# Attention scores on two 64-row halves of the tensor array, three products each, in place of stacked queries and keys

## The chip, the cores and the metric

One core of a Trainium2 chip runs the whole program in one launch. The metric is the device time of one execution in microseconds (us). The kernel before was timed three times: 920.41, 920.97 and 925.29 us, median 920.97 us.

## The reference, cut to what matters

Three blocks follow one another. The change is in the first.

```python
def _attn_ref(q, k, v, w1, b1, w2):          # q, k, v: (4, 8, 576, 64)
    scores = scale * np.matmul(q, k.transpose(0, 1, 3, 2))
    ...                                      # bias[i, j, head] from a small network on positions
    scores = scores + bias.transpose(2, 0, 1)[None, :, :, :]
    scores = scores - np.max(scores, axis=-1, keepdims=True)
    attn = np.exp(scores)
    attn = attn / (np.sum(attn, axis=-1, keepdims=True) + 1e-09)
    return np.matmul(attn, v)

def _moe_ref(x, w1, w2, w3, w_out):          # x: (2304, 512), inner width 1024
    return ((x @ w1) * (x @ w2) @ w3) @ w_out

def _moe2_ref(x, w_in, w_out, g_ln):
    ...                                      # softmax-weighted hidden layer, layer norm, product
```

A score sums over 64 numbers, half the 128 rows of the tensor array. There are 4 x 8 = 32 pictures of 576 x 576 scores.

## The kernel before, in words

Every float32 operand of a product is split into a rounded part (hi) and a rest (lo) of the type float32r, and a product is made of hi·hi, hi·lo and lo·hi (`Chip.three`, lines 76 to 81).

**The stages.** `Bias.run` makes the bias table and stores it in DRAM (to about 59.7 us). `Attention` follows, then `Gated` (the first two-matrix block) and `Solu`. `Attention` works on 16 pairs `n`, each two heads of one batch, head pair outermost. One pair is 10 slots; `slot(s)` writes the instructions of slot `s`, pair `s // 10`, step `k = s % 10`. The engines work in the order in which slots write to them, so this order is a schedule by hand.

**One pair.** Nine units of 128 query rows are scored: unit 0 holds the last 64 rows of both heads ("ends"), units 1 to 4 the other rows of head 0, units 5 to 8 those of head 1. Per unit: scores into a two-bank PSUM tile `sp` (two buffers); `add_bias` on DVE (L381) reads `sp` and a bias tile `bt`, writes `e` and the row minimum; `exp` on ACT (L388); `inverse` on DVE (L395, L396); `normalise` on POOL (L400). `transposes` (L410) turns 128 x 128 blocks of `e` on PE into `tp`, or, for the piece called C, into an `sp` tile with a 128 x 64 array tile. ACT rounds the result (L484), DVE takes the rest (L498), and `values` (L453) multiplies by the values into `op`, which ACT copies out (L486) and SP stores to `x_d`. In slot `s` stand the scores of unit `k`, the transposes that lag by 8 slots (`LAG`) and the values that lag by 11.

**Preparation.** For the next pair, `prep` splits queries and keys on POOL: `qh` (L54), `ql` (L57), `kr` hi and lo (L54, L57), one step per slot in slots 0 to 3; steps 4 and 5 split the values in slots 5 and 6 of their own pair. SP then copies (`move`, L51) into stacked tiles: `q` holds, per head, qh over ql in 128 rows; `k` holds the head's keys twice. With those, one 128-row product sums two of the partial products, so a unit needs two products per half of 288 keys: hi keys and lo keys against the stack (L370), four in all:

```python
for half in range(2):
    for x in range(2):
        nc.tensor.matmul(
            ps[:, half, :HS], w["q"][:, h, q * 128 : q * 128 + 128], w["k"][:, h, x, half * HS : half * HS + HS],
            start=x == 0, stop=x == 1,
        )
```

The keys of head 1 are turned by 64 columns in the copy, since its scores lie turned in `e`. Unit 0 uses `qh`, `ql` and `kr` directly with `Chip.three`.

**After the last scores.** `tile_kernel` runs slots 160 to 174 with `ga.early(n)`, n = s - 160, beside them: weight conversions on ACT and DVE, loads of `x`, and the first products of `Gated` at n = 7, 10 and 14 (`EARLY`). At n = 8 (`MID`) the memory of `e` is given up and the second token chunk is loaded from `x_d` into it (16 DMAs `wf<-x_d`).

Of the kernel before, what the change touches and what calls it, by code (L numbers as in the profile page):

```python
# [17 lines left out]
S = 576  # L18
# [184 lines left out]
class Attention:  # L203
# [52 lines left out]
    def first_ab(self):  # L256

        chains = []
        wab = self.bp.tile([128, 2, S], F, tag="bt", name="wab", bufs=6)
        for f in range(2):  # L260
            x = wab[:, f, :DM]

            def out(f=f, x=x):
                if f == 0:
                    self.ga.first = self.ga.big(1)
                self.ch.load(self.ga.first[:, f].bitcast(F), x)

            chains.append(self.ch.f64_steps(self.ga.raw_ab[:, f].rearrange("p (n t) -> p n t", t=2), x) + [out])
        return [step for steps in zip(*chains) for step in steps]
# [10 lines left out]
    def load_qk(self, n):  # L280
        p, b = self.pairs[n]
        w = self.W.setdefault(n, {})
        w["qkr"] = self.qk.tile([128, 1216], F, tag="qkr", name="qkr")
        self.ch.load(w["qkr"], self.i["qk"][b, p])
# [7 lines left out]
    def prep(self, n, step, s):  # L292

        ch, w = self.ch, self.W[n]
        tl = lambda nm, sh, bufs=1: self.qk.tile(sh, R, tag=nm, name=nm, bufs=bufs)
        qr, kr = w["qkr"][:, :640], w["qkr"][:, 640:]

        def copies(dst, top, bottom):
            for h in range(2):
                r = slice(64 * h, 64 * h + 64)  # L300
                for d, src in ((dst[0:64, h], top[r]), (dst[64:128, h], bottom[r])):
                    self.at(s, lambda d=d, src=src: ch.move(d, src))

        def turned(dst, src):

            for h in range(2):
                r = slice(64 * h, 64 * h + 64)
                for a in (0, 64):
                    d = dst[a : a + 64, h]
                    for d, x in ((d[:, :, 64:], src[r, :, :512]), (d[:, :, :64], src[r, :, 512:])) if h else ((d, src[r]),):  # L310
                        self.at(s, lambda d=d, x=x: ch.move(d, x))

        if step == 0:
            w["qh"] = tl("qh", [128, 640])
            ch.pool_round(w["qh"], qr)
        elif step == 1:
            w["ql"] = tl("ql", [128, 640])
            ch.pool_rest(w["ql"], qr, w["qh"])
            w["q"] = tl("q", [128, 2, 512], 2)
            copies(w["q"], w["qh"][:, :512], w["ql"][:, :512])  # L320
        elif step == 2:
            w["kr"] = tl("kr", [128, 2, S])
            ch.pool_round(w["kr"][:, 0], kr)
        elif step == 3:
            ch.pool_rest(w["kr"][:, 1], kr, w["kr"][:, 0])
            w["k"] = tl("k", [128, 2, 2, S], 2)
            turned(w["k"], w["kr"])
        elif step == 4:
            w["v"] = self.ep.tile([128, 10, 128], R, tag="v", name="v", bufs=2)
            ch.pool_round(w["v"][:, :, 0:64], w["vr"])  # L330
        else:
            ch.pool_rest(w["v"][:, :, 64:128], w["vr"], w["v"][:, :, 0:64])

    def load_bias(self, p, *ks):
# [8 lines left out]
        if (p, "pair", pair) not in self.BT:  # L343
            self.BT[(p, "pair", pair)] = self.bp.tile([128, 2, S], F, tag="bt", name="bt", bufs=6)
# [10 lines left out]


    def scores(self, n, k):
        nc, w = self.nc, self.W[n]
        ps = self.sps.tile([128, 2, 512], F, tag="sp", name="sp")
        h, q = (1, k - 5) if k > 4 else (0, k - 1)  # L360
        if k == 0:

            for half in range(2):
                keys = [w["kr"][:, x, half * HS : half * HS + HS] for x in range(2)]
                self.ch.three(ps[:, half, :HS], [w[x][:, 512:640] for x in ("qh", "ql")], keys, True, True)
            e = w["eab"] = self.tp.tile([128, S], F, tag="eab", name="eab", bufs=2)
        else:
            for half in range(2):
                for x in range(2):
                    nc.tensor.matmul(  # L370
                        ps[:, half, :HS], w["q"][:, h, q * 128 : q * 128 + 128], w["k"][:, h, x, half * HS : half * HS + HS],
                        start=x == 0, stop=x == 1,
                    )
            if h == 0:
                w[("e", q)] = self.tp.tile([128, 2, S], F, tag="e", name="e", bufs=8)
            e = w[("e", q)][:, h]
        self.SQ[n * 10 + k] = (n, k, ps, e, self.st[(5 * n + k // 2) % len(self.st)])

    def add_bias(self, n, k, ps, e, st):

        self.nc.vector.tensor_tensor_reduce(  # L381
            out=halves(e), in0=ps[:, :, :HS], in1=halves(self.BT[(self.pairs[n][0], k)]), scale=-0.125, scalar=3e38,
            op0=ALU.add, op1=ALU.min, accum_out=st[:, k % 2 : k % 2 + 1],
        )

    def exp(self, n, k, ps, e, st):
        c = k % 2
        self.nc.scalar.activation(e, e, AF.Exp, bias=st[:, c : c + 1], scale=-1.0, accum_out=st[:, 2 + 2 * c : 3 + 2 * c])  # L388

    def inverse(self, n, k, ps, e, st):  # L390
        if k % 2 == 0 and k < 8:
            return
        c = 1 + k % 2
# [4 lines left out]
    def normalise(self, n, k, ps, e, st):  # L398
        c = 8 + k % 2
# [3 lines left out]
    def transposes(self, n, u):  # L403
# [7 lines left out]
        if u == "AB":  # L411
            for h in range(2):
                w[("et", h)] = [self.ep.tile([128, 4, S], R, tag="et" + x, name="et" + x, bufs=3) for x in "hl"]
            w["etl"] = [self.ep.tile([128, S], R, tag="el" + x, name="el" + x, bufs=2) for x in "hl"]
# [6 lines left out]
        elif u == "C":  # L421
            tr(0, w["eab"][:, 512:])
# [41 lines left out]
    TU = [["AB"], ["C", (0, 0)], [(0, 1)], [(0, 2)], [(0, 3)], ["L"], [(1, 0)], [(1, 1)], [(1, 2)], [(1, 3)]]  # L464
    AV = [(h, c) for h in range(2) for c in range(5)]

    def start(self, n):
        if n < 4:
            self.prep(0, n, -1)
        elif n == 4:  # L470
            self.load_qk(1)
        if n >= 5 and self.later[-1]:
            self.later[-1].pop(0)()

    def slots(self):
        return 10 * len(self.pairs) + self.LAG + 1 + self.AVLAG + 4

    def slot(self, s):
        NP = len(self.pairs)
        n, k = divmod(s, 10)  # L480
        SQ = self.SQ
# [5 lines left out]
        if s - 2 in SQ:  # L487
            self.exp(*SQ[s - 2])
        if s - 1 in SQ:
            self.add_bias(*SQ[s - 1])  # L490
        if s - 3 in SQ:
            self.inverse(*SQ[s - 3])
            if SQ[s - 3][1] % 2:
                self.normalise(*SQ[s - 4])
            if SQ[s - 3][1] % 2 or SQ[s - 3][1] == 8:
                self.normalise(*SQ[s - 3])
        for hi, lo, src in ev:
            self.nc.vector.tensor_tensor(out=lo, in0=src, in1=hi.bitcast(F), op=ALU.subtract)  # L498
        if n < NP and k < 9:
            self.scores(n, k)  # L500
        tn, tu = divmod(s - self.LAG, 10)
        if 0 <= tn < NP:
            for u in self.TU[tu]:
                self.transposes(tn, u)
        an, au = divmod(s - self.LAG - 1 - self.AVLAG, 10)
        if 0 <= an < NP:
            self.values(an, self.AV[au], s)
# [4 lines left out]
        if n < NP:  # L512
            if n + 1 < NP and k < 4:
                self.prep(n + 1, k, s + 1)
            if k in (5, 6):
                self.prep(n, k - 1, s + 1)
# [3 lines left out]
            if p + 1 < NPH:  # L520
                for j in self.AHEAD[min(p, 1)].get((b, k), ()):
# [811 lines left out]
```

## Time and profile before

| what | us |
|---|---|
| median of three runs | 920.97 |
| the profiled execution | 923.45 |
| its span, first to last instruction | 921.7 |
| PE busy in the span | 867.7 (94%) |
| PE weight loads (PEld) busy | 780.2 (85%) |
| DVE busy | 640.6 (70%) |
| ACT busy | 497.5 (54%) |
| POOL busy | 373.0 (40%) |

The shares are of the whole span. A stage has its own limits: between 150 and 300 us, in the middle of the attention, the 50-us windows show PE busy for 49.1 to 49.6 us. Products are pipelined, and a product's row is longer than its step to the next product. PEld is the loading of the stationary operand. Idle time of an engine is put down to what ended it.

### The profile page before, as it was taken

The page shows a single profiled execution, that of the slowest core. Times are in us where ns is not written, and L with a number is a line of the kernel's source. Part 1 is how long each engine was busy: PE and PEld are TensorE (multiplying, and loading weights), DVE is VectorE, ACT ScalarE, POOL GpSimd, SP SyncE. Part 2 cuts the span into 40 slices and gives each one's busy share as a digit, 9 for nine tenths or more (in the row PEclk, how much of TensorE's full clock was granted, in tenths as well). Part 3 has the DMA queues.
Part 4 walks back from the last instruction along what each step waited for, and adds up shares of the span by engine and source line. Part 5 has one row for each costly group of instructions (what it writes and reads, how often), then busy time and mean ns, then how long its engine had stood idle before and what let it go on. Part 6 is the DMA issues. An engine that isn't in the chain of part 4 may idle for free.

```text
span 921.7 us, 16129 instructions
## 1 busy us (share of the span) xinstructions
PE 867.7 (94%) x5430; PEld 780.2 (85%) x5430; DVE 640.6 (70%) x1481; ACT 497.5 (54%) x1052; POOL 373.0 (40%) x432
## 2 busy tenths in 40 slices
PE   7978998999999879979999998999999899999998
PEld 3448998999999769968889898999999688888886
DVE  8887997999999887986663396652445765555552
ACT  7876997899989844433322233232233544444432
POOL 2036887888888650020111024550343532222200
PEclk9997999999999998998999999999999999999999
DMA  6889899998997665654431486663324111111001
GB/s 229 291 281 227 225 269 228 245 276 227 263 285 184 199 197 194 233 204 155 159 115 35 162 284 195 219 215 96 90 89 134 45 46 46 47 46 47 24 23 47
DMA packets 98387, 151.56 MB, mean 164 GB/s; under 512 B 16384, under 2 KB 62848, under 8 KB 98304
## 3 DMA queue, kind: packets, MB, share of 16 engines
q1 hardware_dynamic: 91392, 141.09, 51.6%
q10 hardware_dynamic: 6912, 9.44, 2.9%
q8 instruction: 43, 0.70, 0.3%
q14 instruction: 40, 0.33, 0.1%
HBM read 81.40 MB, written 41.30 MB: 133 GB/s over the span
## 4 chain that ended last, share of the span: by engine, by line
PE 60%; DMA 11%; DVE 8%; SPq 6%; issue 3%; POOL 3%; ACT 3%; ACTq 0%; POOLq 0%; DVEq 0%
PE ab L79 6%; PE ab L80 6%; PE ab L81 6%; DMA k<-kr 4%; PE op L453 4%; SPq L51 4%; PE o L80 4%; PE o L79 4%; PE o L81 4%; PE sp L370 4%; PE x L80 3%; PE tp L410 3%; PE x L81 3%; PE x L79 3%; PE hx L79 2%
## 5 line engine op out<-in xcount | busy, mean ns | idle before, releaser
L79 PE MATMUL ab<-xh,ab 128*128 128x384 f32 x320 | 109.7, 343 | 6.6 <-DVE a L777 4.6
L80 PE MATMUL ab<-xl,ab 128*128 128x384 f32 x320 | 108.9, 340 | 0.0
L498 DVE TENSOR_TENSOR etl<-tp,eth 128x512 fp32r<-128x512 f32 (+1 forms) x160 | 99.4, 630 | 13.4 <-ACT eth L484 10.9
L81 PE MATMUL ab<-xh,ab 128*128 128x384 f32 x320 | 108.7, 340 | 0.0
L400 POOL TENSOR_SCALAR e<-e,st 128x576 f32<-128x576 f32 x128 | 95.4, 756 | 30.9 <-DVE st L396 28.7
L370 PE MATMUL sp<-k,q 128*128 128x288 f32 x512 | 91.9, 304 | 12.5 <-DMA k<-kr 5.9
L388 ACT ACTIVATE e<-e,st 128x576 f32<-128x576 f32 x128 | 100.2, 783 | 5.3 <-DVE st L381 5.2
L381 DVE CUSTOM_DVE_ANT_0 e<-sp,bt 128x576 f32<-128x576 f32 x128 | 95.6, 748 | 8.0 <-PE sp L370 6.4
L484 ACT CAST eth<-tp 128x512 fp32r<-128x512 f32 (+1 forms) x160 | 85.2, 543 | 26.5 <-PE tp L410 19.9
L410 PE MATMUL tp<-idt,e 128*128 128x128 f32 x576 | 88.9, 277 | 4.2 <-DVE ell L498 2.0
L729 POOL TENSOR_TENSOR xs<-xh,xl 128x384 f32<-128x384 f32 x20 | 23.0, 1162 | 172.0 <-DMA xl<-x_d 97.2
L370 PEld LDWEIGHTS sp<-k,q 128*128 128x128 f32 x512 | 77.1, 194 | 15.0 <-DVE st L381 6.3
L410 PEld LDWEIGHTS tp<-idt,e 128*128 128x128 f32 x576 | 70.8, 143 | 6.9 <-DVE ell L498 2.3
L80 PE MATMUL x<-gl,wf 128*128 128x384 f32 x192 | 66.5, 346 | 6.0 <-DVE gl L62 5.9
L79 PEld LDWEIGHTS ab<-xh,ab 128*128 128x128 f32 x320 | 61.1, 191 | 9.4 <-DVE a L777 6.3
L453 PE MATMUL op<-eth,v 128*128 128x288 f32 x256 | 66.3, 340 | 0.4 <-ACT o L486 0.4
L79 PE MATMUL x<-gh,wf 128*128 128x384 f32 x192 | 65.7, 342 | 0.0
L81 PE MATMUL x<-gh,wf 128*128 128x384 f32 x192 | 65.6, 342 | 0.0
L1157 POOL TENSOR_TENSOR st<-st,half 128x1 f32<-128x1 f32 x18 | 10.0, 554 | 131.9 <-DVE st L1156 131.9
L80 PEld LDWEIGHTS ab<-xl,ab 128*128 128x128 f32 x320 | 61.1, 191 | 0.4 <-DVE xl L738 0.4
L81 PEld LDWEIGHTS ab<-xh,ab 128*128 128x128 f32 x320 | 61.1, 191 | 0.0
L777 DVE TENSOR_TENSOR a<-ab,a 128x384 f32<-128x384 f32 x48 | 26.5, 552 | 47.9 <-ACT a L776 47.9
(207 smaller groups left out, 2288.3 us busy)
## 6 DMA issues: line engine op xcount, KB each, us to landing
bias_d<-rs SPq DMA_DIRECT2D x36, 295.5 KB, 4.2
qkr<-in_qk SPq DMA_DIRECT2D x16, 608.0 KB, 5.7
k<-kr SPq DMA_DIRECT2D x32, 288.0 KB, 6.6
x_d<-o SPq DMA_DIRECT2D x64, 144.0 KB, 4.1
g_d<-a ACTq DMA_DIRECT2D x48, 192.0 KB, 2.8
gl<-g_d SPq DMA_DIRECT2D x48, 192.0 KB, 2.7
k<-kr SPq DMA_DIRECT2D x32, 256.0 KB, 6.7
raw<-in_wo SPq DMA_DIRECT2D x16, 512.0 KB, 5.1
```

Of the source, the lines that this page charges most:

```text
L51: self.nc.sync.dma_start(out.bitcast(F), in_.bitcast(F))
L79: mm(out, a[0], b[0], start=first, stop=False, skip_group_check=more)
L80: mm(out, a[0], b[1], start=False, stop=False, skip_group_check=more)
L81: mm(out, a[1], b[0], start=False, stop=last, skip_group_check=more)
L370: nc.tensor.matmul(ps[:, half, :HS], w["q"][:, h, q * 128 : q * 128 + 128], w["k"][:, h, x, half * HS : half * HS + HS], start=x == 0, sto ...
L381: self.nc.vector.tensor_tensor_reduce(out=halves(e), in0=ps[:, :, :HS], in1=halves(self.BT[(self.pairs[n][0], k)]), scale=-0.125, scalar=3e38,
L388: self.nc.scalar.activation(e, e, AF.Exp, bias=st[:, c : c + 1], scale=-1.0, accum_out=st[:, 2 + 2 * c : 3 + 2 * c])
L400: self.nc.gpsimd.tensor_scalar(out=e, in0=e, scalar1=st[:, c : c + 1], scalar2=1.0, op0=ALU.mult, op1=ALU.mult)
L410: tr = lambda c, src: nc.tensor.transpose(ps[: src.shape[1], c * 128 : c * 128 + 128], src, self.idt)
L453: nc.tensor.matmul(w["op"][:, half, :HS], lhs, rhs, start=c == 0 and x == 0, stop=c == 4 and x == 1)
L484: self.nc.scalar.copy(hi, src)
L498: self.nc.vector.tensor_tensor(out=lo, in0=src, in1=hi.bitcast(F), op=ALU.subtract)
```

## The change

Scores of head 0 and head 1 of the same 128 query rows are made together. `q` and `k` are now simply hi and lo of both heads, head 0 in partitions 0 to 63 and head 1 in 64 to 127, as POOL writes them; the stacked copies and all `move` DMAs of `prep` are gone. Each head's products use a 64 x 128 tile of the array, at row 0 or row 64, and there are three partial products per half and head: 12 products of 64 rows per two units, where there were 8 of 128 rows. Keys are padded by 64 columns at the host (load of 1280 columns in place of 1216) so that both turns are slices. Units are renumbered (1, 3, 5, 7 head 0; 2, 4, 6, 8 head 1).

Scores now stand in the even slots 2, 4, 6 and 8 (two units each, both `sp` buffers), unit 0 in slot 0, and `add_bias` in the odd slots. The lags become tables: transposes from 10 slots behind, values from 15, so the last values of pair n stand in slot 4 of pair n + 2. The steps of `prep` are put in other slots by `SPLITS`. Bias tiles have 8 buffers in place of 6 and are loaded by another `AHEAD`; `first_ab` converts in place, with no DMA to another tile. The run-out has slots 160 to 176, `MID` is 12 and `EARLY` 7, 14 and 16.

```diff
-    LAG = 8
-    AVLAG = 2
...
-    AHEAD = ({(2, 5): (1,), (3, 3): (0,), (3, 4): (3,), (3, 6): (5,), (3, 8): (7,)}, {(2, 3): (1,), (2, 7): (3,), (3, 3): (0,), (3, 5): (5,), (3, 8): (7,)})
+    AHEAD = {(0, 7): (1,), (1, 7): (5,), (2, 7): (3,), (3, 3): (0,), (3, 7): (7,)}
...
         if step == 0:
-            w["qh"] = tl("qh", [128, 640])
-            ch.pool_round(w["qh"], qr)
+            w["q"] = tl("q", [128, 2, 640])
+            ch.pool_round(w["q"][:, 0], qr)
         elif step == 1:
-            w["ql"] = tl("ql", [128, 640])
-            ch.pool_rest(w["ql"], qr, w["qh"])
-            w["q"] = tl("q", [128, 2, 512], 2)
-            copies(w["q"], w["qh"][:, :512], w["ql"][:, :512])
+            ch.pool_rest(w["q"][:, 1], qr, w["q"][:, 0])
         elif step == 2:
-            w["kr"] = tl("kr", [128, 2, S])
-            ch.pool_round(w["kr"][:, 0], kr)
+            w["k"] = tl("k", [128, 2, S + 64])
+            ch.pool_round(w["k"][:, 0], kr)
         elif step == 3:
-            ch.pool_rest(w["kr"][:, 1], kr, w["kr"][:, 0])
-            w["k"] = tl("k", [128, 2, 2, S], 2)
-            turned(w["k"], w["kr"])
+            ch.pool_rest(w["k"][:, 1], kr, w["k"][:, 0])
...
+    def scores(self, n, c):
+
         nc, w = self.nc, self.W[n]
+        e = w[("e", c)] = self.tp.tile([128, 2, S], F, tag="e", name="e", bufs=8)
+        ps = [self.unit(n, 2 * c + 1 + h, e[:, h]) for h in range(2)]
+        for half in range(2):
+            for t, (x, y) in enumerate(((0, 0), (0, 1), (1, 0))):
+                for h in range(2):
+                    r = slice(64 * h, 64 * h + 64)
                     nc.tensor.matmul(
+                        ps[h][:, half, :HS], w["q"][r, x, c * 128 : c * 128 + 128], w["k"][r, y, 64 - 64 * h + half * HS : 64 - 64 * h + half * HS + HS],
+                        start=t == 0, stop=t == 2, tile_position=(64 * h, 0),
                     )
...
+    TURNS = {0: ["C"], 2: ["AB"], 3: [(0, 0)], 4: [(0, 1)], 5: [(0, 2)], 6: [(0, 3)], 7: ["L"], 8: [(1, 0)], 9: [(1, 1)], 10: [(1, 2)], 11: [(1, 3)]}
+    VALUES = {5 + x: (x // 5, x % 5) for x in range(10)}
+    EXPS = {2: 0, **{u + 3: u for u in (1, 3, 5, 7)}, **{u + 3: u for u in (2, 4, 6, 8)}}
+    SUMS = {3: 0, 6: 1, 8: 3, 10: 5, 12: 7}
+    SCALES = {3: 0, **{u + 5: u for u in range(1, 9)}}
+    SPLITS = {4: (0, 4), 5: (0, 5), 0: (1, 0), 1: (1, 2), 6: (1, 1), 8: (1, 3)}
...
-        return 10 * len(self.pairs) + self.LAG + 1 + self.AVLAG + 4
+        return 10 * len(self.pairs) + 17
...
-    EARLY = {7: (0, 0), 10: (0, 1), 14: (1, 0)}
-    MID = 8
+    EARLY = {7: (0, 0), 14: (0, 1), 16: (1, 0)}
+    MID = 12
```

How the rows stand on PE in the middle of a pair, before (L370 scores, L410 transposes, L453 values; one slot and the start of the next):

```order
L370 MATMUL sp<-k,q 128x288 x4
L410 MATMUL tp<-idt,e 128x128 x4
L453 MATMUL op<-elh,v 128x288 x2
L453 MATMUL op<-ell,v 128x288 x2
L370 MATMUL sp<-k,q 128x288 x4
```

and in the change (L349, L384 and L427 are the same three; two slots, from slot 4 of a pair):

```order
L349 MATMUL sp<-k,q 128x288 x12
L384 MATMUL tp<-idt,e 128x128 x4
L427 MATMUL op<-elh,v 128x288 x2
L427 MATMUL op<-ell,v 128x288 x2
L384 MATMUL tp<-idt,e 128x128 x4
L427 MATMUL op<-eth,v 128x288 x2
L427 MATMUL op<-etl,v 128x288 x2
L349 MATMUL sp<-k,q 128x288 x12
```

Scores come every second slot, for two units at once; the rows with `elh` and `ell` in slot 4 are the last values of the pair two before.

On POOL before, from the split of the next pair's queries to the values' rests (names in brackets are the semaphores waited for; DMAHW are those of DMA queues, DVE_49, PE_49, Activation_49 and Pool_49 those of engines; L400 is `normalise`):

```order
L54 TENSOR_SCALAR qh<-qkr 128x640 [waits DMAHW2_49,DMAHW6_49,DMAHW0_49,PE_49]
L400 TENSOR_SCALAR e<-e,st_940 128x576 [waits DVE_49,Activation_49]
L57 TENSOR_TENSOR ql<-qkr,qh 128x640 [waits DMAHW1_49,DMAHW3_49,PE_49,Pool_49]
L54 TENSOR_SCALAR kr<-qkr 128x576 [waits DMAHW3_49,DMAHW4_49,DMAHW2_49,DMAHW7_49,DMAHW1_49,DMAHW0_49]
L57 TENSOR_TENSOR kr<-qkr,kr 128x576 [waits Pool_49]
L400 TENSOR_SCALAR eab<-eab,st_941 128x576 [waits DVE_49,Activation_49]
L400 TENSOR_SCALAR e<-e,st_941 128x576 [waits Activation_49]
L54 TENSOR_SCALAR v<-vr 128x10x64 [waits DMAHW2_49,PE_49]
```

and in the change, from the split of a pair's values in slot 4 to the split of the next pair's queries in slot 10 (L374 is `normalise`):

```order
L54 TENSOR_SCALAR v<-vr 128x10x64 [waits DMAHW3_49,PE_49]
L57 TENSOR_TENSOR v<-vr,v 128x10x64 [waits Pool_49]
L374 TENSOR_SCALAR e<-e,st_929 128x576 [waits DVE_49,Activation_49]
L57 TENSOR_TENSOR q<-qkr,q 128x640
L374 TENSOR_SCALAR e<-e,st_929 128x576 [waits Activation_49]
L374 TENSOR_SCALAR e<-e,st_930 128x576 [waits DVE_49,Activation_49]
L57 TENSOR_TENSOR k<-qkr,k 128x640
L374 TENSOR_SCALAR e<-e,st_930 128x576 [waits Activation_49]
L374 TENSOR_SCALAR e<-e,st_925 128x576 [waits DVE_49,Activation_49]
L54 TENSOR_SCALAR q<-qkr 128x640 [waits DMAHW1_49,PE_49]
```

The rests of the next pair's queries and keys have moved behind the split of the values, and the keys' rest is the last before the next pair. `v` has two buffers, so its split in slot 4 of a pair waits for PE's values of the pair two before, which the tables now put in the same slot.

## Rows read from the trace of the kernel before

**Rows 1.** Busy time by engine, eight pairs (pair 7's ends to pair 15's); PEclk is the clock.
```profile
core 0: us, PE busy (x) PEld busy (x) DVE busy (x) ACT busy (x) POOL busy (x), PEclk, DMA share, GB/s
173.64:296.06 122.42, 120.43 (x954) 118.34 (x953) 112.53 (x329) 111.59 (x266) 105.56 (x120) 1.00 0.95 255
```

**Rows 2.** Weight loads (PEld) of one slot, in order of time: start us, us.
```profile
149.83 0.59 PEld L370 LDWEIGHTS sp<-k,q 128*128 128x128 f32 x4
150.36 0.49 PEld L410 LDWEIGHTS tp<-idt,e 128*128 128x128 f32 x4
150.81 0.30 PEld L453 LDWEIGHTS op<-eth,v 128*128 128x128 f32 x2
...
151.31 0.19 PEld L370 LDWEIGHTS sp<-k,q 128*128 128x128 f32 x1
```

**Rows 3.** First product of unit 0 of pairs 0, 1, 2, 5, 6, 7 and 15, in order of time.
```profile
59.77 0.37 PE L79 MATMUL sp<-kr,qh 128*128 128x288 f32 x1 [0.18 <-ACT rs L198]
...
74.71 0.59 PE L79 MATMUL sp<-kr,qh 128*128 128x288 f32 x1
...
93.78 0.29 PE L79 MATMUL sp<-kr,qh 128*128 128x288 f32 x1
...
139.23 0.29 PE L79 MATMUL sp<-kr,qh 128*128 128x288 f32 x1
...
158.56 0.29 PE L79 MATMUL sp<-kr,qh 128*128 128x288 f32 x1
...
173.64 0.29 PE L79 MATMUL sp<-kr,qh 128*128 128x288 f32 x1
...
296.06 0.29 PE L79 MATMUL sp<-kr,qh 128*128 128x288 f32 x1
```

**Rows 4.** Waits of PE between 59.7 and 160 us: in total, times, longest.
```profile
PE sp L370 <- DMA k<-kr: 5.2, 2, 2.8
```

**Rows 5.** DMA between 150 and 300 us: issues, KB each, us to landing.
```profile
k<-kr SPq DMA_DIRECT2D x20, 288.0 KB, 6.7
k<-kr SPq DMA_DIRECT2D x20, 256.0 KB, 6.7
```

**Rows 6.** Products of the bias stage with 32-column tiles: xcount | busy us, mean ns.
```profile
L191 PE MATMUL ps<-mk,cf 128*32 128x512 f32 x40 | 10.0, 810 | 1.2 <-DVE mk L162 1.2
```

**Rows 7.** PE around piece C of a pair, in order of time: start us, us.
```profile
157.22 0.42 PE L453 MATMUL op<-etl,v 128*128 128x288 f32 x2
157.48 0.27 PE L410 MATMUL sp<-idt,eab 128*64 128x128 f32 x1
157.59 0.60 PE L410 MATMUL tp<-idt,e 128*128 128x128 f32 x4
```

**Rows 8.** Groups between 150 and 300 us, ten pairs: xcount | busy us, mean ns | idle before.
```profile
L400 POOL TENSOR_SCALAR e<-e,st 128x576 f32<-128x576 f32 x80 | 59.4, 753 | 19.4 <-DVE st L396 18.6 <-ACT o L486 0.7
L381 DVE CUSTOM_DVE_ANT_0 e<-sp,bt 128x576 f32<-128x576 f32 x79 | 59.0, 747 | 0.1
...
L57 POOL TENSOR_TENSOR v<-vr,v 128x640 fp32r<-128x640 f32 x10 | 15.8, 1582 | 0.0
...
L57 POOL TENSOR_TENSOR ql<-qkr,qh 128x640 fp32r<-128x640 f32 x9 | 14.1, 1572 | 0.0
...
L396 DVE RECIPROCAL st<-st 128x2 f32<-128x2 f32 (+1 forms) x50 | 8.3, 166 | 5.2
...
L54 POOL TENSOR_SCALAR v<-vr 128x640 fp32r<-128x640 f32 x10 | 7.3, 732 | 0.0
```

**Rows 9.** The run-out, in order of time: slot 160 on PE, `MID` on SP, the second chunk's products.
```profile
312.42 0.60 PE L410 MATMUL tp<-idt,e 128*128 128x128 f32 x4
...
329.62 9.37 SPq L47 DMA_DIRECT2D wf<-x_d  x16
...
349.53 0.53 PE L79 MATMUL ab<-wf,ab 128*128 128x384 f32 x1
```

More of the change, by code (lines that the diff above doesn't have):

```diff
@@ L258, in first_ab @@
         chains = []
-        wab = self.bp.tile([128, 2, S], F, tag="bt", name="wab", bufs=6)
         for f in range(2):
[L261 to L268, printed above, removed]
+            raw = self.ga.raw_ab[:, f].rearrange("p (n t) -> p n t", t=2)
+            chains.append(self.ch.f64_steps(raw, self.ga.raw_ab[:, 2 + f, :DM].bitcast(F)))
         return [step for steps in zip(*chains) for step in steps]
@@ L354, in load_bias, with unit @@
             self.bias.read(t[:, :, :64], row, 2 * p + 1, 512)
-    def scores(self, n, k):
-        nc, w = self.nc, self.W[n]
[L359 to L369, printed above, removed]
+    def unit(self, n, u, e):
+        ps = self.sps.tile([128, 2, 512], F, tag="sp", name="sp")
+        self.SQ[(n, u)] = (u, ps, e, self.st[(5 * n + (u + 1) // 2) % len(self.st)], self.BT[(self.pairs[n][0], (u + 1) // 2 + 4 - 4 * (u % 2) if u else 0)])
+        return ps
@@ L381, in add_bias @@
+                        start=t == 0, stop=t == 2, tile_position=(64 * h, 0),
+                    )
+    def add_bias(self, u, ps, e, st, bias):
+        c = u % 2 == 0 and u > 0
         self.nc.vector.tensor_tensor_reduce(
[L382 to L387 removed]
+            out=halves(e), in0=ps[:, :, :HS], in1=halves(bias), scale=-0.125, scalar=3e38,
+            op0=ALU.add, op1=ALU.min, accum_out=st[:, c : c + 1],
+        )
@@ L421, in transposes @@
         elif u == "C":
+            w["etl"] = [self.ep.tile([128, S], R, tag="el" + x, name="el" + x, bufs=2) for x in "hl"]
             tr(0, w["eab"][:, 512:])
@@ L486, in slot @@
             self.nc.scalar.copy(*self.OUT.pop())
[L487 to L496, printed above, removed]
+        for m, x in rounds:
+            if x in self.EXPS:
+                self.exp(*self.SQ[(m, self.EXPS[x])])
+        if n < NP and k % 2:
+            for u in (0,) if k == 1 else (k - 2, k - 1):
+                self.add_bias(*self.SQ[(n, u)])
+        for m, x in rounds:
+            if x in self.SUMS:
+                self.inverse(*self.SQ[(m, self.SUMS[x])])
+            if x in self.SCALES:
+                self.normalise(*self.SQ[(m, self.SCALES[x])])
         for hi, lo, src in ev:
             self.nc.vector.tensor_tensor(out=lo, in0=src, in1=hi.bitcast(F), op=ALU.subtract)
[L499 to L507, printed above, removed]
+        if n < NP and k == 0:
+            self.ends(n)
+        elif n < NP and k % 2 == 0:
+            self.scores(n, k // 2 - 1)
+        for m, x in rounds:
+            for u in self.TURNS.get(x - 10, ()):
+                self.transposes(m, u)
+        for m, x in rounds:
+            if x - 10 in self.VALUES:
+                self.values(m, self.VALUES[x - 10], s)
         if k == 4 and n + 2 < NP:
```

78 lines of the change are left out of this document (31 added, 47 removed).

## The prediction

> **What bounds the kernel now.** I read the busy time by engine first, then one slot in order of time, then the spacing of the pairs. In eight pairs in the middle of the attention [rows 1] PE is busy for 120.4 of 122.4 us, at full clock; DVE (112.5), ACT (111.6) and POOL (105.6) are close behind. So PE bounds this stage, and little is to be had before another engine does: per pair DVE works 112.53 / 8 = 14.07 us and POOL 13.2 us.
>
> One slot [rows 2] runs from load to load: four scores 0.53 us (0.1325 a product), four transposes 0.45, four value products 0.50; in all 1.48. A pair is then 8 x 0.53 for units 1 to 8, 6 x 0.1325 for unit 0, one product for C and ten times 0.95: 14.67 us. Measured from one pair's first product to the next [rows 3], a quiet pair takes 15.08 (158.56 to 173.64), the mean of pairs 7 to 14 is 122.42 / 8 = 15.30, and two are long: pair 1 19.07 and pair 5 19.33. In that time PE waited 5.2 us directly for the copied keys [rows 4], and every pair moves over 1 MB of key copies through the queue [rows 5]. All 15 periods together are 296.06 - 59.77 = 236.3 us.
>
> **The change part by part.**
>
> *Scores.* Per pair 32 products of 128 rows become 48 of 64 rows, in 24 couples that lie on different halves of the array and write different PSUM banks. The trace has no 64-row tile. The low bound for a couple is one product's step, 0.1325; the high bound is two steps, 0.265. The nearest rows are the bias stage's products on 32-column tiles [rows 6]: 40 products of 512 columns last 0.81 us each and fill only 10.0 us, so about 3.2 run at a time, and four tiles take 1.0 us, little more than one. In the ordinary stream a row of 0.29 with a step of 0.1325 gives 2.2. I take the low bound: 24 x 0.1325 = 3.18 in place of 4.24. PE falls from 14.67 to 13.61 us a pair.
>
> *Switches between tile shapes*, two at each group of scores, eight a pair. The trace holds such a switch at piece C, a 128 x 64 tile between 128 x 128 ones [rows 7]: its product starts 0.13 after the last value product at 157.35 (157.22 plus one step), and the next follows after 0.11. That is no longer than any step, so I cost a switch at nothing. The Trainium skill, TensorEngine Tiling (Array Packing), section Tiling Modes, speaks against it: "Changing tiling mode (not just tile) drains the TensorE". By that rule the sum would be some 10 to 18 us worse; the trace disagrees for the column tile of C, and no row shows it for row tiles.
>
> *DVE, ACT.* They keep every instruction. DVE's 14.07 plus the wait before each of five reciprocals, 5.2 / 50 = 0.10 [rows 8], is 14.6 a pair, which is the floor if nothing else binds. Inside two slots it holds: two `add_bias` (1.5) follow the scores, and PE has 2 x 0.95 of other work meanwhile.
>
> *POOL, the step I choose as the new bound.* Its work grows by some 0.2 us a pair (two key instructions 64 columns wider), to 13.4: not a bound by itself. Its place is. The split of the values in slot 4 now waits for the value products that PE makes in that slot for the pair two before, the last readers of that buffer. Behind it, in order, stand the values' rest, one `normalise`, the queries' rest, two more `normalise`, the keys' rest; and the second product of the next pair's unit 0 needs those keys. So a ring closes once a pair. On PE, from that product to the end of slot 4: five products of unit 0 (0.66), C (0.13), five slots of transposes and values (4.75), two groups of scores (1.59): 7.13, and 0.16 until the last product's row ends (0.29 less its step). On POOL [rows 8]: 0.73 + 1.58 + 3 x 0.75 + 2 x 1.57 = 7.70. Sum 14.99; with two hand-overs I take 15.1 us (an estimate). That is above DVE's 14.6 and PE's 13.6, and equal to the quiet pair of now. The ring exists from pair 2 on, as the first two find the two buffers free.
>
> *Copies gone.* Ten DMAs a pair leave SP's queue, and with them the wait of rows 4. I let both long pairs go. What is late next is the ring.
>
> *First pairs.* Pair 0 keeps its 14.94 (74.71 - 59.77): its bias tiles come as late as before, and it has no transposes. Pair 1 takes 14.6 in place of 19.07. Pairs 2 to 14 take 13 x 15.1 = 196.3. Sum 225.8 in place of 236.3: 10.5 less. Pair 15, with no next pair to prepare, reaches slot 160 after 14.6 in place of 312.42 - 296.06 = 16.4 [rows 9]: 1.8 less.
>
> *Run-out.* The loads of the second chunk need the memory of `e`, whose last transposes move from slot 167 to 171. Before, eight slots took 329.62 - 312.42 = 17.2 us, 2.15 each, and the second chunk's products stood 19.9 us after the loads' start [rows 9], a chain of 16 DMA issues, sums and splits that does not change. Four more slots cost at most 8.6. At least they cost the work that comes over from earlier slots: six sets of transposes and five of values, 6 x 0.45 + 5 x 0.50 = 5.2. I take the middle, 6.9. PE is busy behind it, so nothing hides this.
>
> *Sum* against the profiled execution: 923.45 - 10.5 - 1.8 + 6.9 = 918.0 us. That execution was 2.5 us above the median, so for a median of runs I predict 915.5.
>
> **The rivals.**
>
> *The ring does not bind* (POOL's `normalise` of the next pair or the end of slot 4 falls earlier than reckoned): 14.6 a pair, 13 x 0.5 = 6.5 less, 909. For it: POOL is idle for 17 us in rows 1. Against: the order on POOL and its durations leave no room that I found. With the run-out at its low bound 907; I go down to 905.
>
> *The long pairs stay*, since the wait was for a full DMA queue and not the copies, or a late bias tile takes their place: 8 us back, 923.5. Against: the copies are most of what the queue holds [rows 5], and rows 4 name them.
>
> *A switch costs, or weights load in single file.* If each switch lets the last product's row end (0.16) and perhaps the next load follow it (0.11, the transposes' step), the ring has four of them: 0.64 to 1.1 a pair. If two half loads of 128 columns can't lie side by side, each of the 12 products of a group takes at least the shortest step of the trace, 0.45 / 4 = 0.11: a group is 1.35 in place of 0.80 and the ring 1.1 longer. Either gives 13 x 0.64 to 1.1, and 1.4 to 3.2 more in pairs 1 and 15: 925 to 933. For it: no row shows 64-row tiles. The Trainium skill, TensorE: Matmul & The Clock Gate, section LDWEIGHTS (loading the stationary operand), has a load cost by its columns, "not the contraction dim K", so half the rows would save nothing of a load; the transposes' step agrees with a load-bound step of that size, and no run here shows a half load.
>
> *The halves do not run together* (slower; the change then doesn't do what it says). Each product takes its own step: a group is 1.59, PE has 13.61 + 3.18 + the 0.41 by which the quiet pair exceeds its sum = 17.2 a pair, more than the ring (16.7). 13 x 2.1 + 2 x 2.6 = 32.5 and a little in pair 0: 949. It decides from a couple's step of about 0.2 on; up to 0.16 DVE and POOL hide it.
>
> **How the numbers follow.** A measurement of this kernel tells about 0.5% from no change: 916.4 to 925.6. Forecast 0.47 (911 to 919 by the run-out's bounds and the ring's hand-overs, some 0.28 of it under 916.4), ring not binding 0.15, long pairs stay 0.10, switches or loads 0.17, no overlap 0.11. Faster: 0.28 + 0.15 = 0.43. Same: 0.19 + 0.10 = 0.29. Slower: 0.28. The range leaves out the last rival and little else: 905 to 935. The forecast's own range is 911 to 919.
>
> **What would show it.** Two scores of a couple starting together and 12 of them within about 0.8 us, with no gap at the switch. PE idle before the second product of unit 0, ended by POOL's keys' rest (L57), and POOL idle before the split of the values, ended by PE's value products, once in each pair from pair 2. Pairs 15.1 apart, none of 19. No waits of PE for a DMA of keys. The loads of the second chunk some 23 to 26 us after slot 160. The prediction is wrong if pairs stand 14.6 apart (no ring) or 16 and more (no overlap), or if the run-out loses what the pairs gain.

## The result, and the profile after

The changed kernel took **932.28 us** (median of four, 931.10 to 935.47) where the kernel before took 920.69 (median of four, 920.31 to 925.29): a ratio of 1.0136, 95% interval 1.0097 to 1.0175. It is slower by 1.4%, which is clear of the noise; 915.5 was forecast. The range of the prediction (905 to 935) holds the time, its most likely direction is wrong.

Eight pairs of the changed kernel (first product of pair 7's unit 0 to that of pair 15), by engine, as in [rows 1]:

```profile
core 0: us, PE busy (x) PEld busy (x) DVE busy (x) ACT busy (x) POOL busy (x), PEclk, DMA share, GB/s
168.29:298.33 130.04, 127.69 (x1082) 112.48 (x1081) 116.14 (x329) 110.35 (x266) 106.84 (x121) 1.00 0.42 121
```

The copies are gone as planned: the DMA share falls from 0.95 to 0.42. But eight pairs take 130.04 us in place of 122.42, at the same granted clock of 1.00 (its 2.4 GHz level), and PE is still busy for 98% of it. DVE is busy 3% longer, POOL 1%.

First product of unit 0 of pairs 0, 1, 2, 6, 7 and 15 on PE, in order of time, as in [rows 3]:

```profile
57.49 0.37 PE L79 MATMUL sp<-k,q 128*128 128x288 f32 x1 [0.18 <-ACT rs L198]
...
71.35 0.58 PE L79 MATMUL sp<-k,q 128*128 128x288 f32 x1 [0.72 <-DVE st L357]
...
87.02 0.29 PE L79 MATMUL sp<-k,q 128*128 128x288 f32 x1
...
152.05 0.29 PE L79 MATMUL sp<-k,q 128*128 128x288 f32 x1
...
168.29 0.29 PE L79 MATMUL sp<-k,q 128*128 128x288 f32 x1
...
298.33 0.29 PE L79 MATMUL sp<-k,q 128*128 128x288 f32 x1
```

No pair takes 19 us any more: pair 1 takes 15.66, and from pair 2 on each takes 16.2 to 16.3, on average 16.25 ((298.33 - 152.05) / 9, pairs 6 to 14). The 15 periods sum to 240.84; 225.8 was forecast, and before they took 236.3. The spans differ by 930.5 - 921.7 = 8.8 us: the pairs give 4.5 of it, the time from pair 15's unit 0 to the end 6.6 (632.2 against 625.6), and the first pair starts 2.3 us earlier (in the profiles of the experiments that begin as the change does it starts at 56.8 to 59.1 us, so part of this is the spread between executions). The other 2.8 of the 11.6 between the medians are what the profiled execution before (923.45) lay above its median.

One group of scores and its neighbours on PE, in order of time, then the loads of the same stretch:

```profile
181.20 0.42 PE L427 MATMUL op<-etl,v 128*128 128x288 f32 x2
181.55 1.07 PE L349 MATMUL sp<-k,q 64*128 64x288 f32 x12
182.55 0.65 PE L384 MATMUL tp<-idt,e 128*128 128x128 f32 x4
182.96 0.51 PE L427 MATMUL op<-eth,v 128*128 128x288 f32 x2
183.31 0.43 PE L427 MATMUL op<-etl,v 128*128 128x288 f32 x2
183.58 0.60 PE L384 MATMUL tp<-idt,e 128*128 128x128 f32 x4
...
186.02 0.27 PE L384 MATMUL sp<-idt,eab 128*64 128x128 f32 x1
186.04 0.51 PE L427 MATMUL op<-eth,v 128*128 128x288 f32 x2
```

```profile
181.07 0.32 PEld L427 LDWEIGHTS op<-etl,v 128*128 128x128 f32 x2
181.55 0.83 PEld L349 LDWEIGHTS sp<-k,q 64*128 64x128 f32 x12 [0.16 <-issue]
182.55 0.42 PEld L384 LDWEIGHTS tp<-idt,e 128*128 128x128 f32 x4 [0.17 <-issue]
182.93 0.30 PEld L427 LDWEIGHTS op<-eth,v 128*128 128x128 f32 x2
```

Two things are to be seen. The 12 products take 1.00 us from first to next (181.55 to 182.55), which 12 single steps of 0.1325 (1.59) could not: **the halves do run together**. And the loads have gaps of 0.16 and 0.17 us at the two switches, where elsewhere a load starts while the products before it still run: the first load of the scores starts with its own product, 0.35 after the last two value products began (two value products followed by transposes: 0.27, from 183.31 to 183.58). Piece C's column tile between full tiles still shows no cost: from the transposes ahead of it to the values behind it 0.46 us pass (185.58 to 186.04), 0.10 more than for four transposes alone (0.36), and one transpose more would take 0.11.

Step by step, worked out from the start times of PE's rows, mean of pairs 6 to 13 (a step ends where the next begins):

```
us                          before  after   without copies*  last version*
unit 0, 6 products            0.79   1.04        0.79            0.79
scores of one unit, 4 full    0.53     -         0.53             -
scores, slot 2                  -    1.32          -             0.99
scores, slots 4, 6, 8, each     -    0.99          -             1.00
4 transposes, plain           0.35   0.36        0.35            0.36
the same behind scores          -    0.41          -             0.41
4 values, then transposes       -    0.61          -             0.61
4 values, then scores         0.61   0.70        0.61            0.70
transposes of slot 5            -    0.89          -             0.36
one pair                     15.31  16.25       15.03           15.16
```
(* experiments below; "full" are products on the whole array.) Six couples alone would be 6 x 0.1325 = 0.80. A group takes 0.99, the values ahead of it 0.09 more than elsewhere and the transposes behind it 0.055 more: **a switch out and back costs 0.20 + 0.09 + 0.055 = 0.34 us**, four times a pair 1.4. Of the 0.20, 0.11 lie between the first couple and the second and 0.09 between the last couple and the transposes; the couples between follow one another every 0.13.

The waits of the eight pairs (us in total, times, longest):

```profile
POOL v L54 <- PE op L427: 12.2, 8, 1.5
...
PEld op L427 <- ACT o L462: 4.3, 8, 0.5
PE op L427 <- ACT o L462: 2.3, 8, 0.3
PEld sp L80 <- POOL k L57: 1.7, 8, 0.2
```

POOL waits 1.5 us a pair for PE's values before it splits the values, and PE waits for the keys' rest once a pair: the ring of the prediction is there, though PE's wait in it is only 0.2. A wait that nobody forecast is larger: the values of slot 5 need the `op` buffer, which ACT copies out late (L462); the transposes' step ahead of them is 0.89 in place of 0.36.

One passage of the ring: unit 0's second product, the end of slot 4's values, POOL's first and last instruction in it, and the second product of the next unit 0:

```profile
184.81 0.19 PEld L80 LDWEIGHTS sp<-k,q 128*128 128x128 f32 x1 [0.21 <-POOL k L57]
...
192.87 0.43 PE L427 MATMUL op<-ell,v 128*128 128x288 f32 x2
...
193.39 0.73 POOL L54 TENSOR_SCALAR v<-vr 128x640 fp32r<-128x640 f32 x1 [1.53 <-PE op L427]
...
199.44 1.58 POOL L57 TENSOR_TENSOR k<-qkr,k 128x640 fp32r<-128x640 f32 x1
...
201.08 0.19 PEld L80 LDWEIGHTS sp<-k,q 128*128 128x128 f32 x1 [0.20 <-POOL k L57]
```

POOL's half, from 193.39 to 201.02, takes 7.63 (7.70 forecast). PE's half, from unit 0's second product (184.81) to the end of slot 4's values (193.3), takes 8.5, where 7.29 was forecast. With hand-overs of 0.09 and 0.06 the two make 16.27 us, the whole period: **the ring closes without slack, at 16.25 and not at 15.1.** The wait for `op`, in slot 5, lies outside it.

### The profile page after: what moved, and what is told of

The parts are those of the page before. It is cut to its first block, busy times and chain, and to the rows that moved or that the text cites. A ratio compares the mean times of both kernels' runs of the same rounds, so it can differ in the third digit from the quotient of the medians.

```text
span 930.5 us, 16215 instructions
## 1 busy us (share of the span) xinstructions
PE 874.7 (94%) x5686; PEld 762.9 (82%) x5686; DVE 643.4 (69%) x1481; ACT 493.3 (53%) x1052; POOL 380.6 (41%) x432
## 4 chain that ended last, share of the span: by engine, by line
PE 75%; DVE 7%; DMA 4%; issue 4%; ACT 4%; SPq 1%; POOL 0%; ACTq 0%; DVEq 0%; POOLq 0%
PE op L427 9%; PE tp L384 8%; PE sp L349 7%; PE ab L79 6%; PE ab L80 6%; PE ab L81 6%; PE o L80 4%; PE o L79 4%; PE o L81 4%; PE x L80 3%; PE x L81 3%; PE x L79 3%; PE hx L79 2%; PE hx L80 2%; PE hx L81 2%
## 5 line engine op out<-in xcount | busy, mean ns | idle before, releaser
L374 POOL TENSOR_SCALAR e<-e,st 128x576 f32<-128x576 f32 x128 | 96.1, 765 | 12.4 <-ACT eth L460 8.2
L357 DVE CUSTOM_DVE_ANT_0 e<-sp,bt 128x576 f32<-128x576 f32 x128 | 91.5, 752 | 4.7 <-PE sp L349 4.7
L707 POOL TENSOR_TENSOR xs<-xh,xl 128x384 f32<-128x384 f32 x20 | 26.3, 1323 | 162.7 <-DMA xl<-x_d 146.4
L384 PE MATMUL tp<-idt,e 128*128 128x128 f32 x576 | 89.3, 278 | 3.0 <-DVE etl L475 2.7
L349 PE MATMUL sp<-k,q 64*128 64x288 f32 x768 | 77.2, 318 | 5.1 <-DVE st L357 5.0
L384 PEld LDWEIGHTS tp<-idt,e 128*128 128x128 f32 x576 | 67.0, 141 | 12.1 <-issue 7.7
L349 PEld LDWEIGHTS sp<-k,q 64*128 64x128 f32 x768 | 58.6, 190 | 19.4 <-issue 8.4
L79 PEld LDWEIGHTS ab<-xh,ab 128*128 128x128 f32 x320 | 60.1, 188 | 14.9 <-DVE a L755 11.9
L427 PE MATMUL op<-eth,v 128*128 128x288 f32 x256 | 65.4, 337 | 6.6 <-ACT o L462 6.6
L81 PEld LDWEIGHTS ab<-xh,ab 128*128 128x128 f32 x320 | 60.1, 188 | 0.0
```

What stands on the lines that cost most here:

```text
L79: mm(out, a[0], b[0], start=first, stop=False, skip_group_check=more)
L81: mm(out, a[1], b[0], start=False, stop=last, skip_group_check=more)
L349: nc.tensor.matmul(ps[h][:, half, :HS], w["q"][r, x, c * 128 : c * 128 + 128], w["k"][r, y, 64 - 64 * h + half * HS : 64 - 64 * h + half * ...
L357: self.nc.vector.tensor_tensor_reduce(out=halves(e), in0=ps[:, :, :HS], in1=halves(bias), scale=-0.125, scalar=3e38, op0=ALU.add, op1=ALU. ...
L374: self.nc.gpsimd.tensor_scalar(out=e, in0=e, scalar1=st[:, c : c + 1], scalar2=1.0, op0=ALU.mult, op1=ALU.mult)
L384: tr = lambda c, src: nc.tensor.transpose(ps[: src.shape[1], c * 128 : c * 128 + 128], src, self.idt)
```

## The experiments

**The theory** after the result: switches and three waits make 16.25 out of the 13.61 us of products. Rivals: the switch as measured is partly something else; the halves overlap only by their order of issue; one wait only stands for another. In brackets behind a time stand its ratio to runs of the kernel before that were taken beside it, and the 95% interval.

### What a switch costs

*One more switch.* Between the two halves of a group stands a small product on the full array (its result is never read); in a second kernel the same product on a 64-row tile (`z = slice(0, 64)` and `tile_position=(0, 0)`). Their difference is a switch out and back, four a pair, 64 in all.

```diff
+            if half:
+                z = slice(0, 128)
+                nc.tensor.matmul(ps[0][:, 0, 384:448], w["q"][z, 0, c * 128 : c * 128 + 128], w["k"][z, 0, 0:64], start=True, stop=True)
```

> The change with one small full-array product (64 columns, into unused columns of the bank) between the two halves of each group of scores: one more change of tile shape out and back per group. Theory: its own step plus some 0.35 us a group, 1.4 us a pair, over e2b_same_shape: 20 to 25 us more than e2b_same_shape. Rival (shapes change for nothing, the gaps are waits for buffers): within 3 us of e2b_same_shape.

> The control: the same small product on the upper 64-row tile, so no change of shape. Both theories: at most one step, 0.13 us a group, 0.5 us a pair: 932 to 941 us.

Full array 963.07 us (ratio to before 1.0492, 1.0441 to 1.0544), 64 rows 938.97 (1.0230, 1.0149 to 1.0310): 24.1 us apart, 0.38 for each of 64, from two runs each (those of the second are 4.8 us apart). Pairs took 17.93 and 16.58: 1.35 us, 0.34 each. PE, the group of slot 2 in the first and in the second (from its second product on, which waits for a buffer):

```profile
185.64 0.63 PE L352 MATMUL sp<-k,q 64*128 64x288 f32 x5 [0.22 <-DVE ell L478]
186.20 0.30 PE L348 MATMUL sp<-k,q 128*128 128x64 f32 x1
186.43 0.66 PE L352 MATMUL sp<-k,q 64*128 64x288 f32 x6
```

```profile
173.43 0.63 PE L352 MATMUL sp<-k,q 64*128 64x288 f32 x5 [0.20 <-DVE ell L478]
173.80 0.19 PE L348 MATMUL sp<-k,q 64*128 64x64 f32 x1
173.82 0.63 PE L352 MATMUL sp<-k,q 64*128 64x288 f32 x6
```

From the small product to the next score 0.23 us pass where the shape changes, and 0.02 where it doesn't (the other half goes on beside it). With the shape unchanged a group of slots 4, 6 and 8 is 0.11 longer than in the changed kernel (1.10), with the switch 0.42 (1.41). So the switch is priced by itself: 0.31 to 0.34 us out and back.

*No switch.* Six full-array products in place of six couples.

```diff
-            for t, (x, y) in enumerate(((0, 0), (0, 1), (1, 0))):
-                for h in range(2):
...
+            for h, (x, y), first, last in ((0, (0, 0), True, False), (0, (0, 1), False, True), (1, (1, 0), True, True)):
+                nc.tensor.matmul(
+                    ps[h][:, half, :HS], w["q"][:, x, c * 128 : c * 128 + 128], ...
```

> Six full-array products per group of scores in place of the 12 on half arrays: as many steps on PE, no change of tile shape (it leaves out keeping the heads apart, so the scores are not the reference's). Theory (a change of tile shape costs some 0.35 us a group, 1.4 us a pair): PE's own sum falls from 16.05 to 14.65 and the ring through POOL, shorter by two groups' switches, is left: pairs 15.2 to 15.5 apart, 917 to 921 us. Rival (the pace of 16.25 is set by waits of the new order, not by the switches): pairs 16 and more, 929 us or more.

926.40 us (1.0066, 1.0035 to 1.0097), 15.84 a pair: 0.41 was won where 0.75 to 1.05 was expected. The groups of slots 6 and 8 fall to 0.79, but unit 0 grows from 1.04 to 1.74. Waits from 180 to 290 us, seven pairs:

```profile
PEld sp L80 <- POOL k L57: 6.3, 7, 0.9
PE sp L80 <- POOL k L57: 4.7, 7, 0.7
```

The time lies between the theory's 917 to 921 and the rival's 929. Without switches the ring still closes, at 15.84, since PE's half of it keeps a wait at slot 2 (1.01 in place of 0.79) and now holds one of 0.38 ahead of slot 4's transposes, for DVE's rest. So taking out the switches alone gives back 0.41 of the 1.15 us by which a pair missed the forecast.

*Order of the couples.* Head 0's three products ahead of head 1's.

```diff
-            for t, (x, y) in enumerate(((0, 0), (0, 1), (1, 0))):
-                for h in range(2):
+            for h in range(2):
+                for t, (x, y) in enumerate(((0, 0), (0, 1), (1, 0))):
```

> The change with the three products of head 0 ahead of the three of head 1 in each half, in place of couples. If two tiles run side by side wherever neighbours in the order lie on different halves, 12 products take 9 steps in place of 6: 0.4 us a group, 1.6 a pair, 950 to 960 us. If order does not matter (each half has a queue of its own), no change, 932. If couples were only started together but shared their time, no change either.

933.08 us (1.0165, 1.0110 to 1.0221; two runs), 16.29 a pair: no change. The scores' products between 180 and 290 us, xcount | busy us, mean ns, in this kernel and in the changed one:

```profile
L349 PE MATMUL sp<-k,q 64*128 64x288 f32 x324 | 31.3, 308 | 0.0
```

```profile
L349 PE MATMUL sp<-k,q 64*128 64x288 f32 x324 | 30.9, 310 | 0.0
```

Neighbours in the order need not be on different halves; the theory of overlap by order falls.

### What the waits cost

*No ring.* The next pair's splits ahead of the split of the values.

```diff
-    SPLITS = {4: (0, 4), 5: (0, 5), 0: (1, 0), 1: (1, 2), 6: (1, 1), 8: (1, 3)}
+    SPLITS = {0: (1, 0), 1: (1, 2), 2: (1, 1), 4: (1, 3), 5: (0, 4), 6: (0, 5)}
```

> The change with the next pair's rests first on POOL (slots 2 and 4) and the split of the values in slots 5 and 6, behind PE's last reader of the buffer: no ring. Theory (switches): PE loses only the 0.2 us a pair that it waits for the keys' rest, pairs 16.0 apart, some 3 us less, 929. Rival (the ring sets the pace): pairs 15 apart or less, 915 or less.

934.41 us (1.0158, 1.0097 to 1.0218), 16.25 a pair: nothing gained, and neither the 929 nor the 915 that were expected. Unit 0 falls to 0.79, and slot 2's scores grow from 1.32 to 1.55. Its waits of 180 to 290 us:

```profile
PE op L427 <- ACT o L462: 1.8, 6, 0.3
PE sp L349 <- DVE ell L475: 1.5, 7, 0.2
```

The second is the score buffer that piece C holds until DVE's rest. *Both edits (no switch, no ring):*

> Both edits. Theory: DVE is left, 14.6 to 14.8 us a pair, some 21 us less than the change: 910 to 914. If the ring was no bound even without switches, the same as e1_no_switch within 3 us.

918.52 us (0.9967, 0.9938 to 0.9996), 15.19 a pair. Beside the kernel without the ring this is 1.06 us a pair and 16 us; beside the one without switches 0.65 and 8. So of these four kernels the ring is worth something only where the switches are gone. The expected 910 to 914 is missed: slot 2's scores take 1.31 and slot 4's 1.16 (0.79 without a wait), and slot 5's transposes 0.89.

*Reordered:* no ring, ACT's output copy ahead of its casts, and C's transposes first.

> The change with no ring (as e3_no_ring), ACT's copy of the output ahead of its casts in a slot, and piece C ahead of the older pair's transposes, so that PE's waits for op and for the second sp buffer shrink. Theory: 0.2 + 0.5 + 0.3 us a pair less, pairs 15.2 to 15.5 apart, 918 to 921 us: level with the kernel before. If the waits only move, 926 to 932.

934.59 us (1.0151, 1.0090 to 1.0211), 16.20 a pair: a miss. Slot 2's scores fall to 0.99, but the casts now stand behind the output copy, the values of slot 0 take 0.90, slot 4's scores 1.21, and the transposes of slot 5 still 0.89: the wait for `op` did not go.

*Values early:* the last values of a head-1 set one slot earlier, so that ACT's copy lies under slot 4.

```diff
-    VALUES = {5 + x: (x // 5, x % 5) for x in range(10)}
+    VALUES = {5 + x: [(x // 5, x % 5)] + [(1, 4)] * (x == 8) for x in range(9)}
...
```

> The changed kernel, with the last values of a head-1 set one slot earlier: slot 3 has two sets of values, slot 4 none. The same work in another order. ACT's copy of the output then lies under slot 4, so PE's wait for it in slot 5 (some 0.54 us a pair) goes, and the split of the values finds its buffer free a slot earlier, so the ring goes too (0.2 us). If the waits add up, a pair takes 15.5 to 15.7 and the time is 921 to 924 us. If they only move to the next buffer, as in the kernel with the reordered slots, a pair stays at 16.1 to 16.25 and the time at 930 to 933.

927.66 us (1.0075, 1.0046 to 1.0105), 15.80 a pair: slot 5's transposes fall from 0.89 to 0.36, and the pair by 0.45; the time lies between the two forecasts. PE's wait for the keys' rest did not go (unit 0 takes 1.15), though POOL's split no longer waits for PE. The edit also brings the last reader of `v` forward and so shortens PE's half of the ring; that the `op` wait counts by itself is shown by the next kernel beside the one without the ring. *With the ring out as well:*

> The same, with the splits of the next pair also put ahead of the split of the values, as in the kernel without the ring. If PE's work with its switches is then what is left, a pair takes 13.61 + 1.4 = 15.0 to 15.3 us and the time is 912 to 918 us. If the wait moves to the scores of slot 2 for their buffer, as in the kernel without the ring, a pair takes 15.6 or more: over 921 us.

927.24 us (1.0080, 1.0052 to 1.0107), 15.74 a pair: unit 0 falls by 0.36 to 0.79, and slot 2's scores rise by 0.29 to 1.56. The wait for C's buffer takes the ring's place. Beside the kernel without the ring (16.25, slot 2 the same) a pair is 0.51 shorter: that is the wait for `op`.

*C in unit 0's score tile*, in its unused columns, so that it holds no buffer; on the kernel above, and on the changed one.

```diff
-            ps = self.sps.tile([128, 2, 512], F, tag="sp", name="sp")[:, 0]
+            ps = self.SQ[(n + 1, 0)][1][:, 0, 384:]
```

> The kernel with the values early and no ring, with C's product written into the unused columns of unit 0's score tile (columns 384 to 511 of its first bank), so that C takes no score buffer of its own. There the scores of slot 2 took 1.56 us in place of 0.99 and nothing else stood out. If they wait for the buffer that C holds, 0.5 to 0.57 us a pair goes: 15.2 a pair and 918 to 920 us. If they wait for the bias addition of unit 0 or the wait moves on, a pair stays above 15.5 and the time above 923.

> The changed kernel with that edit alone. By the theory of a ring that sets the pair's length (POOL's splits wait for the values of slot 4, PE's unit 0 for the keys), an earlier slot 2 is given back at unit 0 only if nothing in the ring gets shorter; slot 2 lies inside the ring, so up to 0.33 us a pair goes: 15.9 and 926 to 928 us. If the waits of slots 2, 5 and 0 stand for one another, a pair stays at 16.2 and the time at 931 to 933.

940.95 us (1.0242, 1.0206 to 1.0278) and 947.48 (1.0308, 1.0271 to 1.0346): 14 to 15 us slower than the kernels that they were made from. The first falls under the open end of its second forecast, the second under none. Slot 2's scores take 2.53 and 2.30. The bias addition of unit 0 now waits for ACT's cast of C, most likely because both read one tile; in the changed kernel it starts ahead of that cast (169.54 against 170.48). DVE, the first of the two:

```profile
209.19 0.76 DVE L357 CUSTOM_DVE_ANT_0 eab<-sp,b 128x576 f32<-128x576 f32 x1 [1.31 <-ACT elh L460]
```

*C first:* values early, no ring, and C ahead of the other transposes of its slot, so that its buffer comes free earlier.

```diff
-        for m, x in rounds:
+        for m, x in reversed(rounds):
             for u in self.TURNS.get(x - 10, ()):
```

> The kernel with the values early and no ring, and C's transposes ahead of the other transposes of their slot, so that ACT and DVE read C first and its score buffer comes free earlier for slot 2. If that buffer is the last wait, slot 2's scores fall from 1.56 to about 1.0, a pair takes 15.2 (13.61 of products as forecast and 1.4 of switches, with 0.15 over) and the time is 918 to 920 us. If the values of slot 0 then wait for their own rests instead, as in the kernel with the reordered slots (0.3 us), a pair takes 15.5 and the time is 923 to 925.

**918.11 us** (0.9969, 0.9944 to 0.9995), 15.16 a pair: the expected value. It leaves out no part of the computation, and beats the changed kernel by 1.5% and the kernel before by 0.3% (the interval ends just short of no change). Its eight pairs:

```profile
163.78:285.08 121.30, 121.30 (x1082) 110.73 (x1081) 113.24 (x329) 109.90 (x266) 106.29 (x120) 1.00 0.47 133
```

PE's rows fill all of it, and no step stands out any more: 13.61 of products as forecast, 1.4 of switches, and 0.15 that the forecast's steps leave out.

### What the copies cost, and the run-out

*The kernel before without its copies.*

```diff
...
-            copies(w["q"], w["qh"][:, :512], w["ql"][:, :512])
...
-            turned(w["k"], w["kr"])
...
-                        ps[:, half, :HS], w["q"][:, h, q * 128 : q * 128 + 128], w["k"][:, h, x, half * HS : half * HS + HS],
+                        ps[:, half, :HS], w[("qh", "ql")[h]][:, q * 128 : q * 128 + 128], w["kr"][:, x, half * HS : half * HS + HS],
```

> The kernel before without its copies: POOL's hi and lo of queries and keys (two buffers each) are read directly by the scores, four products of 128 rows a unit as before (what they sum is no longer one head's score, so the scores are not the reference's). If the two long pairs come from the copies, they go, and 19.07 + 19.33 less 2 x 15.1 = 8.2 us with them: about 912 to 914 us. If a late bias tile holds those pairs, they stay: 919 to 922. If the copies also slow the quiet pairs, a pair falls under 15.08 and the time under 911.

908.87 us (0.9871, 0.9832 to 0.9909), 15.03 a pair and no long pair. The copies cost 11.5 us, somewhat more than the 8.2 of the two long pairs: five others, of 15.3 to 15.75, fall to 15.03 as well. So the stacked products are the shorter of the two forms: 32 steps (4.24) against 24 couples and four switches (3.18 + 1.4 = 4.58). Of that 0.34 us the pair shows 0.13, since the transposes of slot 1 still wait there (0.54 in place of 0.35). The gain of the change was all in the copies.

*The run-out.* Loads of the second chunk on SP: 338.16 in the changed kernel, 39.8 us after pair 15's unit 0; before, 329.62, 33.6 us after it.

```profile
338.16 7.67 SPq L47 DMA_DIRECT2D wf<-x_d  x16
```

Fewer weight conversions beside the last slots, on the kernel with C first and on the changed one:

```diff
-            self.convert(2 if n < 9 else 3)
+            self.convert(1 if n < 12 else 5)
```

> The kernel with C first, and in the run-out one weight conversion step a slot until the loads of the second chunk, and five a slot behind them, in place of two and then three. In that kernel slots 163 to 171 take about 2.1 us each, and DVE's rows between the rests are conversion steps of 0.68 to 1.0 us, two a slot. If they set the slots' pace, up to 9 x 0.6 = 5 us of the run-out goes, since the loads of the second chunk come that much earlier: 913 to 915 us. If the chain of cast, rest and transposes sets it, or the next block then waits for the conversions that came later, nothing goes: 917 to 921.

> The changed kernel with that edit alone. If DVE's conversion steps set the pace of the run-out, the same 4 to 5 us: 927 to 928. If not, 931 to 934.

923.98 us (1.0039, 1.0018 to 1.0061) and 937.19 (1.0171, 1.0129 to 1.0212), 6 and 5 us slower, which neither forecast had. The loads don't come earlier (325.35 for 323.76 in the first, 338.16 again in the second): the conversions don't set the pace of these slots, and later they are missed (in the second, PE then waits 10.6 us for weights that ACT converts, 4.4 in the changed kernel). What sets it, most likely the chain of cast, rest and transposes of the added slots, wasn't isolated.

## Why the prediction failed

- **The steps that failed: "I cost a switch at nothing", and the size of PE's half of the ring (7.29) that followed from it and from leaving out a wait.** The free switch of [rows 7] is that of C, a 128 x 64 tile, and I took it for the 64-row tile. For C it still holds after the change; for 64 rows out and back is 0.34 us, by a pair of kernels that differ only in the shape of one small product. Four a pair over 16 pairs are 64 x 0.34 = 22 us of PE's work. The Trainium skill, TensorEngine Tiling (Array Packing), section Tiling Modes, whose rule I had weighed and set aside, has a change of tiling mode drain the engine. The trace agrees for the row tiles, where the loads have gaps of 0.16 and 0.17 us, and disagrees for C's column tile; that the gaps are a drain is not shown.
- **Switches are not the whole miss.** My pace was the ring's, 15.1, and 13.61 of products with 1.4 of switches, 15.0, would still have fitted under it. PE's half of the ring measured 8.5: 0.68 more by the switches of two groups, 0.33 by slot 2's wait for the score buffer that C holds, which I had put at nothing without a reason, and 0.2 by unit 0 and smaller steps. Without switches the kernel takes 926.40 us, still above the kernel before; with the switches and without the waits it takes 918.11. Of the 16.8 us between 915.5 and 932.28 the switches alone give back 5.9 and the waits alone 14.2. The two overlap, so these are not shares.
- **The rivals.** "A switch costs" came true in its first half, but its 925 to 933 holds 932.28 partly by luck: at the measured 0.17 for one switch, four in the ring are 0.68, its low end, and the waits did the rest. Its second half, loads in single file, did not: two half loads run side by side, and 12 take 0.83 us. My sign for no overlap, pairs 16 and more, came true with the halves overlapping.
- **Couples, right.** The low bound of 0.1325 holds: inside a group couples follow one another every 0.13 us, and of the 0.99 that a group takes, 0.20 is the switch.
- **Copies, right**, and rather more than forecast.
- **The ring, right in its mechanism and wrong in its size.** POOL's half measured 7.63 (7.70), the hand-overs 0.15, and the ring closes once a pair. Taken out alone it gives nothing, since a bound of the same length stands behind it: PE's products, the switches, the wait for `op` (0.54) and the wait for C's buffer (then 0.56) make 16.25 too. The wait for `op` (0.51 us a pair by the values moved) I had not seen: I costed ACT at "every instruction kept" and did not ask when its output copy comes.
- **Sum of a pair.** 13.61 products, 1.4 switches, 0.54 for `op`, 0.33 at slot 2, 0.25 at unit 0: 16.13, measured 16.25. In the kernel with C first the last three are gone and the switches are left.
- **First and last stretches.** Pair 1 takes 15.66 (14.6); the run-out with pair 15 lost 6.6 (6.9 - 1.8 = 5.1): pair 15 takes 16.5 to slot 160, not 14.6, as its slots keep PE's switches and waits. Both small. Pair 0 takes 13.86 (14.94), with no wait for a bias tile.

## What to carry to other kernels

Price a switch by the very shapes that it joins: a free switch of one kind says nothing of another, and a product of the same size put between at either shape prices it in two runs. Where a schedule by hand has several buffers that come free just in time, take the waits out together before judging one of them; here the ring alone gave nothing, the values moved (the wait for `op`) 4.6 us, and all three together 14.2. A priced step tells what is lost only together with what else binds: the switches, 22 us of PE's work, gave back 5.9 when they alone were gone. A form with fewer product steps loses if it must change shape around each small group: six couples save two of eight steps (0.27 us) and pay 0.34.

## What the runs showed of the hardware beyond that

- The two 64-row halves overlap whatever the order of issue within a group: three products of one half ahead of three of the other cost nothing (933.08 against 932.28 us), and in that kernel's trace the products still start in couples, 0.01 us apart.
- A switch costs on both sides, at a granted clock of 1.00: about 0.20 us on the way in (last value to first couple 0.22 and first to second couple 0.24, where a step is 0.13) and 0.14 on the way out (last couple to first transpose 0.22 for 0.13, first transpose to the second 0.165 for 0.11).
- A 64-row weight load is no shorter than one of 128 rows (0.19 us, as the last of [rows 2]), but two of them take no longer than one:

```profile
181.55 0.19 PEld L349 LDWEIGHTS sp<-k,q 64*128 64x128 f32 x2 [0.16 <-issue]
```
